# The opening of an attention-then-mixer kernel: which latents are scored first, and where the small copies stand

## The chip, the cores and the metric

The kernel runs on one core of one Trainium2 chip. The metric is device time in microseconds (us) of one execution; the time before is a median of 3 runs. TensorE (PE) multiplies matrices into PSUM, ScalarE (ACT) and VectorE (DVE) move and change results, GpSimd (POOL) and SyncE (SP) here mostly issue DMAs. PEld is TensorE's weight load, which overlaps its matmuls.

## The reference

For each of 8 batches, with sequence length S = 3136, width D = 256 and latent width 64:

```python
scores = (1 / S) * z @ z.T              # z: [8, 3136, 64]
attn   = np.maximum(scores, 0) ** 2
x      = u * (attn @ v)                 # u, v: [8, 3136, 256]
h      = x.transpose(0, 2, 1) @ U @ V   # U: [3136, 32], V: [32, 3136]
y      = x + h.transpose(0, 2, 1)
out    = y + np.maximum(y @ w_ch1, 0) @ w_ch2   # w_ch1: [256, 1024], w_ch2: [1024, 256]
```

## The kernel before

**Tiles.** The 3136 rows are cut into 25 tiles of 128, the last with 64 rows (`NT` = 25, `NF` = 24, `TAIL` = 64). "Latent j" is tile j of z; "output o" is tile o of the result. Since scores are symmetric, for every latent j the kernel keeps only its blocks with the tiles j to j + 12 (cyclically) in `A[j]` (up to 13 blocks of 128 columns); the other 12 blocks that output o needs are a transposed copy of `A[o]`, made by a DMA on SP (`turn`, L398) into a buffer called `strip`.

**A score step** (`score`, L353) takes two halves of a block row. Two matmuls (L360) in different 64-row halves of the array write the two halves of one PSUM pair tile (`pair_psum`, two buffers of two banks). ACT applies the ReLU and the scale into `A` (L378), or DVE does it where the argument `vector` says so (L374), and then DVE squares the block in place (L380). `make_stored` calls `score` for a panel of blocks of two latents; `score_steps` cuts a whole row of `A` into steps.

**An attention step** multiplies blocks by tiles of `v` (`half`, L478), two outputs at a time, accumulating in two sets of two PSUM banks (`sets`). `close_pair` (L487) adds the two banks (an ACT copy, L492, and a DVE sum, L493) and multiplies by `u` (DVE, L510). The tile of `u` comes by a DMA on POOL (`load_u`, L462), into one of two buffers, `u_sb`.

**After a batch**, the low-rank part runs inside the next batch: `rank_sums` (L580), `rank_close` (L592, L594), and `low_rank` (L635), which multiplies a tile of `V_bf` by the rank-32 sums. `V_bf` holds four copies of V in the four 32-row groups, and consecutive matmuls of `low_rank` read its rows 0 to 63 and 64 to 127. In the stretch of outputs of batch 0, the steps in `puts` fill it: DVE writes the first group in six steps (L332, L339) and then two copies (L343) widen it from 32 to 64 and from 64 to 128 rows.

**Order.** The schedule is manual: the program's order is the order of each engine's queue. For the steady state, `attend_steps` gives the matmuls of one output, and `_spread` and `_merge` put the score steps of coming latents between them. The first batch has its own opening, `start_up`, which does outputs 12 to 19 (12 is `FIRST`, 16 is `LEAD`) before the loop over outputs begins with i = 8 (output 20; `turns(i)` is (12 + i) mod 25).

- `first_z` issues dummy matmuls (L269) on a zeroed tile while z arrives, then casts z to bf16, one copy on DVE (L277) and one on ACT (L278). `turn_on_pe` transposes latents on PE with an identity (L285) and copies them out of PSUM into `zT_first` (L293).
- Outputs 12 to 15 are done together: for each entry of `pairs`, `make` scores two latents against tiles 12 to 15 and, two entries later, `use` multiplies those blocks by `v`. Into the gaps go the score steps of latents 16 to 19 (`nxt`), some on DVE (`vector`). The latents 16 to 24 are turned at entry 6.
- Outputs 16 to 19 follow the same way from stored blocks (`make_stored`, `use_stored`). The products by `u` of the first four outputs (`products`) and the loads of the next two pairs of `u` tiles stand between the two groups, followed on POOL by a one-column copy (`mark`, L886), which waits for a strip, and two loads of the next batch's `v`.
- `first_at`, `first_more` and `first_turns` say which score steps and turns go into outputs i = 8 to 14.

```python
        pairs = [(8, 9), (10, 11), (12, 13), (14, 15), (6, 7), (3, 4), (5,), (1, 2)]
        pairs += [(0, 16), (17, 18), (19, 20), (21, 22), (23, 24)]
        ...
        for i, pair in enumerate(pairs):
            ...
            make(pair)
            if i > 5 and i % 2:
                nxt.pop(0)()
            if i > 1:
                use(pairs[i - 2], outs)
```

Of the kernel before, what the change touches and what calls it, by code (L numbers as in the profile page):

```python
# [42 lines left out]
def kernel(  # L43
# [218 lines left out]
    def first_z(parts):  # L262
# [5 lines left out]
        for _ in range(7):  # L268
            mm(out=ps[:, 0, :], lhsT=zT_rest[:, 0, :], rhs=wide, start=True, stop=True)  # L269
        landed = []  # L270
        for t0, t1 in parts:
            z_f = u_pool.tile([P, 2, D], FP32, name="u_sb").rearrange("p a c -> p (a c)")
            z_f = z_f.rearrange("p (t c) -> p t c", c=dqk)
            nc.sync.dma_start(out=z_f, in_=rows(z[0])[:, t0:t1, :])
            landed.append(z_f)
        for (t0, t1), z_f in zip(parts, landed):
            nc.vector.tensor_copy(out=z_bf[:, t0:t1, 0, :], in_=z_f)  # L277
            nc.scalar.copy(out=z_bf[:, t0:t1, 1, :], in_=z_f)  # L278

    def turn_on_pe(parts, banks):  # L280

        z_bf = z_two
        for (t0, t1), ps in zip(parts, banks):
# [8 lines left out]
            copy = nc.vector.tensor_copy if t0 % 8 or t1 == NF else nc.scalar.copy  # L292
# [21 lines left out]
    def weight_steps():  # L314
# [26 lines left out]
        def copies():  # L341
            for n in (R, 2 * R):
                nc.vector.tensor_copy(out=V_bf[n : 2 * n, :], in_=V_bf[:n, :])  # L343
# [4 lines left out]
        return fetches, second_w, puts + [put_tail, copies]  # L348
# [4 lines left out]
    def score(b, parts, vector=False):  # L353
# [18 lines left out]
        for dst, src in todo:  # L372
            if vector:
# [5 lines left out]
        for dst, _ in todo:  # L379
            nc.vector.tensor_tensor(out=dst, in0=dst, in1=dst, op=ALU.mult)  # L380

    def score_steps(b, j, k0=0, k1=NB, vector=()):
# [5 lines left out]
        for i in range(parts):  # L388
            at = k0 * P + i * each

            def step(at=at, i=i):
                dst = A[j][:, at : at + each].rearrange("p (i h) -> p i h", i=2)
                score(b, [(j, j * P + at + k * h, h, dst) for k in range(2)], i in vector)
# [387 lines left out]
    def start_up():  # L781
        parts = ((8, 16), (0, 8), (16, NF))
        first_z(parts[:2])
# [9 lines left out]
        )  # L793
        load_v(0, (8, 12))
        load_v(0, (12, 18))
        load_z(0, parts[2:])
        for part in [(3, 8), (0, 3), (18, NF), (NF, NT)]:
            load_v(0, part)
        turn_on_pe([(8, 12), (12, 16)], sets[0])
        turn_on_pe([(0, 4), (4, 8)], sets[1])  # L800
# [12 lines left out]
        vector = {LEAD: (1,), LEAD + 1: (0,)}  # L813
# [3 lines left out]
        pairs = [(8, 9), (10, 11), (12, 13), (14, 15), (6, 7), (3, 4), (5,), (1, 2)]  # L817
# [3 lines left out]
        def make(pair):  # L821
            if all(LEAD - 1 - HALF <= j < FIRST for j in pair):
# [5 lines left out]
                score(0, todo)  # L828
            else:
# [3 lines left out]
                score(0, [(j, c0, NG * P, room) for j in pair])  # L833
# [8 lines left out]
        for i, pair in enumerate(pairs):  # L842
            if i == 4:
                double_z(parts[2:])
            if i == 6:
                turn_on_pe([(16, NF)], [pair_psum().rearrange("p a w -> p (a w)")])
                turn_on_pe([(NF, NT)], [pair_psum()[:, 0, :]])
                extend_z(0)
            make(pair)
            if i > 5 and i % 2:  # L850
                nxt.pop(0)()
            if i > 1:
                use(pairs[i - 2], outs)
# [28 lines left out]
        run(products)  # L882
        for o in outs[::2]:
            load_u(0, o)
        if B > 1:
            nc.gpsimd.tensor_copy(out=mark, in_=strips[0, LEAD + NG - 1][:, 0, :1])  # L886
            for part in V_PARTS[3:5]:
                load_v(1, part)
# [5 lines left out]
        for i, pair in enumerate(pairs):  # L894
# [5 lines left out]
            if i == len(pairs) - 1:  # L900
                turn(0, LEAD + NG)
        tail = []
# [16 lines left out]
        for s in _merge(tail, more[:-2] + rest[:2] + more[-2:]):  # L919
            s()  # L920
        turn(0, LEAD + 2 * NG - 1)


# [9 lines left out]
    for j, i in zip(range(3, FIRST), (10, 11, 12, 13, 13, 13, 14, 14, 14)):  # L933
        first_at[i].append((j, 0, FIRST - j))
    first_more = {
        8: [((j, j - 1), LEAD + NG) for j in (LEAD - 5, LEAD - 7)] + [((LEAD - 1, LEAD - 2), LEAD + 2 * NG)],
        9: [((LEAD - 3, LEAD - 4), LEAD + 2 * NG)],
    }
    first_turns = {8: (), 9: (24,), 10: (0,), 11: (1,), 12: (2,), 13: (3,), 14: ()}
# [152 lines left out]
```

## Time and profile before

| what | value |
|---|---|
| median of 3 runs | 998.56 us (994.47 to 998.61) |
| the profiled execution | 994.09 us, its span 992.4 us |
| PE busy | 979.3 us (99%), 13632 instructions |
| PEld busy | 814.9 us (82%) |
| ACT busy | 613.9 us (62%) |
| DVE busy | 554.5 us (56%) |
| POOL busy | 170.1 us (17%) |
| granted TensorE clock | 1.000 |

The span runs from the first to the last recorded instruction, and the 1.7 us between it and the execution's time lie around it. A matmul's end is modelled, so a busy PE is not a PE at its peak pace. Idle time of an engine costs something only where the engine that sets the end waits for it. The profile's line numbers are those of the kernel before.

### The profile page before, as it was taken

The numbers are of one execution on the slowest core, as the hardware profiler recorded it, in microseconds if no ns is written. First come the engines' busy times: TensorE is split into PE (matmuls) and PEld (weight loads), VectorE is DVE, ScalarE is ACT, GpSimd is POOL, SyncE is SP. The second block draws the span as 40 slices with busy tenths as digits, with TensorE's granted clock in tenths as the row PEclk, the third lists the DMA queues.
The fourth block names the chain that finished last, engine by engine and source line by source line (L and its number), as shares of the span: only waits on it lengthen the run. The fifth ranks groups of instructions, "written<-read, shape, count | busy, mean of one in ns | idle before, by whom it ended". The sixth has DMA issues, their size and how long they took to land.

```text
span 992.4 us, 31020 instructions
## 1 busy us (share of the span) xinstructions
PE 979.3 (99%) x13632; PEld 814.9 (82%) x13672; DVE 554.5 (56%) x1027; ACT 613.9 (62%) x843; POOL 170.1 (17%) x317
## 2 busy tenths in 40 slices
PE   8899999999999999999999999999999999999998
PEld 5788878888888888788887888878888788788876
DVE  6789835557346574374653655546546466352342
ACT  7879764766647575575755757467574676643154
POOL 5111112112121111212112121121211201111000
PEclk9999999999999999999999999999999999999999
DMA  9999889999799899998987999989889796595443
GB/s 197 175 175 210 149 172 207 176 193 180 140 186 182 164 174 138 194 184 167 171 161 167 187 169 164 164 169 188 160 159 194 157 192 127 126 199 109 89 107 102
DMA packets 399976, 164.42 MB, mean 166 GB/s; under 512 B 375568, under 2 KB 384464, under 8 KB 399840
## 3 DMA queue, kind: packets, MB, share of 16 engines
q1 hardware_dynamic: 371520, 96.14, 61.1%
q0 software_dynamic: 28320, 66.28, 28.1%
q8 instruction: 107, 1.75, 0.7%
q14 instruction: 29, 0.24, 0.1%
HBM read 61.88 MB, written 25.69 MB: 88 GB/s over the span
## 4 chain that ended last, share of the span: by engine, by line
PE 95%; ACT 2%; DVE 2%; issue 0%; DMA 0%; DVEq 0%
PE ps L478 50%; PE ps L714 17%; PE ps L667 17%; PE ps L360 7%; ACT A L378 2%; PE ps L635 1%; PE ps L525 1%; DVE A L380 1%; PE ps L580 1%; DVE x_bf L510 0%; PE ps L269 0%; DMA out_dram<-o_sb 0%; PE ps L285 0%; DVE both L493 0%; ACT both L492 0%
## 5 line engine op out<-in xcount | busy, mean ns | idle before, releaser
L378 ACT ACTIVATE A<-ps 128x832 bf16<-128x832 f32 (+10 forms) x479 | 356.7, 765 | 140.8 <-PE ps L360 135.2
L478 PE MATMUL ps<-v,A 64*128 64x256 bf16 x4988 | 341.2, 269 | 2.5 <-DVE A L380 2.5
L380 DVE TENSOR_TENSOR A<-A 128x832 bf16<-128x832 bf16 (+9 forms) x481 | 243.4, 523 | 131.5 <-ACT A L378 129.1
L478 PE MATMUL ps<-v,strip 64*128 64x256 bf16 x4420 | 309.5, 269 | 0.0
L478 PEld LDWEIGHTS <-A 64*128 64x128 bf16 x4988 | 252.1, 94 | 41.8 <-issue 6.0
L685 ACT ACTIVATE relu_bf<-ps 128x1024 bf16<-128x1024 f32 (+2 forms) x208 | 188.2, 909 | 150.4 <-PE ps L667 144.7
L478 PEld LDWEIGHTS <-strip 64*128 64x128 bf16 x4420 | 227.3, 94 | 30.5
L714 PE MATMUL ps<-w_bf,relu_bf 128*128 128x256 bf16 (+1 forms) x1600 | 201.4, 273 | 0.4
L667 PE MATMUL ps<-ut,w_bf 128*128 128x512 bf16 (+2 forms) x856 | 198.1, 353 | 1.7
L714 PEld LDWEIGHTS <-relu_bf 128*128 128x128 bf16 (+1 forms) x1600 | 153.0, 98 | 40.2 <-issue 4.9
L732 DVE TENSOR_TENSOR o_sb<-ps,x_bf 128x512 f32<-128x512 f32 (+2 forms) x81 | 54.9, 678 | 170.9 <-PE ps L714 164.6
L667 PEld LDWEIGHTS <-w_bf 128*128 128x128 bf16 x896 | 117.9, 144 | 37.4 <-issue 6.7
L360 PE MATMUL ps<-zT 64*128 64x416 bf16 (+8 forms) x812 | 134.8, 312 | 0.0
L462 POOL DMA_DIRECT2D u_sb<-in_u_dram x96 | 53.5, 557 | 453.4 <-DVE x_bf L510 430.5
L492 ACT COPY both<-ps 128x512 f32<-128x512 f32 (+1 forms) x104 | 59.0, 568 | 70.0 <-PE ps L478 63.9
L493 DVE TENSOR_TENSOR both<-ps,both 128x512 f32<-128x512 f32 (+1 forms) x104 | 69.3, 666 | 30.8 <-ACT both L492 30.4
L649 DVE TENSOR_TENSOR x_bf<-ps,x_bf 128x512 bf16<-128x512 f32 (+1 forms) x112 | 65.5, 626 | 11.3 <-PE ps L635 11.2
L510 DVE TENSOR_TENSOR x_bf<-both,u_sb 128x512 bf16<-128x512 f32 (+1 forms) x104 | 69.7, 671 | 3.6
L745 POOL DMA_DIRECT2D out_dram<-o_sb x66 | 36.0, 546 | 187.0 <-DVE o_sb L732 175.0
L360 PEld LDWEIGHTS <-zT 64*128 64x128 bf16 x812 | 46.3, 94 | 3.7
L732 DVE TENSOR_TENSOR both<-ps,x_bf 128x512 f32<-128x512 f32 (+1 forms) x24 | 15.0, 623 | 57.3 <-PE ps L714 57.3
L306 POOL DMA_DIRECT2D v<-in_v_dram x61 | 33.7, 555 | 4.0 <-issue 2.7
(66 smaller groups left out, 244.3 us busy)
## 6 DMA issues: line engine op xcount, KB each, us to landing
u_sb<-in_u_dram POOLq DMA_DIRECT2D x96, 256.0 KB, 4.4
out_dram<-o_sb POOLq DMA_DIRECT2D x66, 256.0 KB, 3.0
v<-in_v_dram POOLq DMA_DIRECT2D x57, 192.0 KB, 4.4
out_dram<-both POOLq DMA_DIRECT2D x18, 256.0 KB, 2.3
strip<-A SPq DMA_TRANSPOSE x194, 5.5
out_dram<-o_sb SPq DMA_DIRECT2D x11, 256.0 KB, 2.1
z_c<-in_z_dram POOLq DMA_DIRECT2D x7, 384.0 KB, 6.7
w_bf<-in_moe_w_ch_dram POOLq DMA_DIRECT2D x2, 512.0 KB, 6.2
```

What stands on the lines that cost most here:

```text
L360: mm(out=ps[:, k, :n], lhsT=zT[halves[k], j + at[k], :], rhs=zT_flat[halves[k], c + at[k] * P : c + at[k] * P + n], start=True, stop=True,)
L378: nc.scalar.activation(out=dst, in_=src, func=AF.Relu, scale=sc)
L380: nc.vector.tensor_tensor(out=dst, in0=dst, in1=dst, op=ALU.mult)
L478: mm(out=acc[t0][h][:, (o - t0) * D : (o - t0 + 1) * D], lhsT=w[halves[h]], rhs=v_both[b % 2][halves[h], j, :], start=start, stop=stop, **kw,)
L492: nc.scalar.copy(out=both[:, :w], in_=banks[1][:, :w])
L493: nc.vector.tensor_tensor(out=both[:, :w], in0=banks[0][:, :w], in1=both[:, :w], op=ALU.add)
L510: nc.vector.tensor_tensor(out=x_at(b, t0, n), in0=split(both[:, :w]), in1=u_sb[:, :n, :].rearrange("p t (a c) -> p t a c", c=P), op=ALU.mult,)
L649: nc.vector.tensor_tensor(out=q, in0=split(ps[h][:, : len(ks) * D]), in1=q, op=ALU.add)
L667: mm(out=ps[i][:, :w] if apart else ps[:, i, :w], lhsT=w1_at[:, db, hp + i, :], rhs=uT[c][:, db, len(chunks[c]) * P - w :], start=(db == 0 ...
L685: nc.scalar.activation(out=relus[c][:, hp : hp + 2, :w], in_=ps[:, :, :w], func=AF.Relu)
L714: mm(out=ps[r, k * D : (k + 1) * D], lhsT=relus[c][:, ht, q : q + (TAIL if two else P)], rhs=w2_bf[:, ht, :], start=(ht < 1 + two), stop=( ...
L732: nc.vector.tensor_tensor(out=o_sb[:p].rearrange("p t (a c) -> p t a c", c=P), in0=split(ps[:p, k0 * D : (k + 1) * D]), in1=x_at(b, t, nk) ...
```

## The change

The change touches the order of work in the opening and the place of two copies; the matmuls that make the result are the same.

- z arrives in three parts instead of two (tiles 12 to 15, 8 to 11, 0 to 7). The tiles 12 to 15 are cast and turned first, then 8 to 11. There is one dummy matmul less.
- The entries (12, 13) and (14, 15) move to the front of `pairs`. The tiles 0 to 7 are cast after the first entry and turned after the second. In the first entry, latent 13 is evicted by DVE from the second half of the pair tile whose first half ACT evicts, and both squares stand behind the cast. The products of the first use are split by pairs of outputs.
- At entry 6, tile 24 is turned first, then 16 to 19 (copied by ACT) and 20 to 23 (by DVE), both into one pair tile.
- At entry 9 the `nxt` step comes ahead of the squares. The second step of latent 18, instead of the first of latent 17, is evicted by DVE.
- The products by `u` of outputs 12 to 15, the two loads of `u`, `mark` and the two loads of `v` move behind the fourth entry of the second group.
- The last steps of the opening: all four panels for outputs 20 to 23 are scored there (two of them came in output i = 8 before); the two steps of latent 23 move to i = 8, and its turn behind it; the panels for 24 to 27 move from i = 8 and 9 to 9 and 10.
- The two copies that widen `V_bf` move from one step at i = 22 of batch 0 to the end of outputs i = 0 and i = 1 of batch 1.

```diff
@@ first_z
-        for _ in range(7):
+        for _ in range(6):
             mm(out=ps[:, 0, :], lhsT=zT_rest[:, 0, :], rhs=wide, start=True, stop=True)
...
+        def cast(n):
+            (t0, t1), z_f = parts[n], landed[n]
             nc.vector.tensor_copy(out=z_bf[:, t0:t1, 0, :], in_=z_f)
             nc.scalar.copy(out=z_bf[:, t0:t1, 1, :], in_=z_f)
@@ weight_steps
-        def copies():
-            for n in (R, 2 * R):
-                nc.vector.tensor_copy(out=V_bf[n : 2 * n, :], in_=V_bf[:n, :])
+        def copies(n):
+            nc.vector.tensor_copy(out=V_bf[n : 2 * n, :], in_=V_bf[:n, :])
@@ score
-        for dst, src in todo:
-            if vector:
+        for n, (dst, src) in enumerate(todo):
+            if n in vector:
...
-        for dst, _ in todo:
-            nc.vector.tensor_tensor(out=dst, in0=dst, in1=dst, op=ALU.mult)
+        def squares():
+            for dst, _ in todo:
+                nc.vector.tensor_tensor(out=dst, in0=dst, in1=dst, op=ALU.mult)
+        if held is None:
+            squares()
+        else:
+            held.append(squares)
@@ start_up
-        parts = ((8, 16), (0, 8), (16, NF))
-        first_z(parts[:2])
+        parts = ((12, 16), (8, 12), (0, 8), (16, NF))
+        on_act, on_dve = nc.scalar.copy, nc.vector.tensor_copy
+        cast = first_z(parts[:3])
...
-        turn_on_pe([(8, 12), (12, 16)], sets[0])
-        turn_on_pe([(0, 4), (4, 8)], sets[1])
+        cast(0)
+        turn_on_pe([(12, 16)], sets[0][:1], [on_act])
+        cast(1)
+        turn_on_pe([(8, 12)], sets[0][1:], [on_dve])
...
-        vector = {LEAD: (1,), LEAD + 1: (0,)}
+        vector = {LEAD: (1,), LEAD + 2: (1,)}
...
-        pairs = [(8, 9), (10, 11), (12, 13), (14, 15), (6, 7), (3, 4), (5,), (1, 2)]
+        pairs = [(12, 13), (14, 15), (8, 9), (10, 11), (6, 7), (3, 4), (5,), (1, 2)]
...
             if i == 6:
-                turn_on_pe([(16, NF)], [pair_psum().rearrange("p a w -> p (a w)")])
-                turn_on_pe([(NF, NT)], [pair_psum()[:, 0, :]])
+                turn_on_pe([(NF, NT)], [pair_psum()[:, 0, :]], [on_act])
+                ps = pair_psum()
+                turn_on_pe([(16, 20), (20, NF)], [ps[:, 0, :], ps[:, 1, :]], [on_act, on_dve])
                 extend_z(0)
-            make(pair)
-            if i > 5 and i % 2:
-                nxt.pop(0)()
+            held = []
+            make(pair, vector=(1,) if i == 0 else (), held=held)
+            if i == 0:
+                cast(2)
+            if i == 1:
+                turn_on_pe([(0, 4), (4, 8)], sets[1], [on_dve, on_act])
+            if i == 9:
+                nxt.pop(0)()
+                run(held)
+            else:
+                run(held)
+                if i > 5 and i % 2:
+                    nxt.pop(0)()
             if i > 1:
-                use(pairs[i - 2], outs)
+                for some in (outs[:2], outs[2:]) if i == 2 else (outs,):
+                    use(pairs[i - 2], some)
...
-        run(products)
-        for o in outs[::2]:
-            load_u(0, o)
-        if B > 1:
-            nc.gpsimd.tensor_copy(out=mark, in_=strips[0, LEAD + NG - 1][:, 0, :1])
-            for part in V_PARTS[3:5]:
-                load_v(1, part)
...
+            if i == 3:
+                run(products)
+                for o in outs[::2]:
+                    load_u(0, o)
+                if B > 1:
+                    nc.gpsimd.tensor_copy(out=mark, in_=strips[0, LEAD + NG - 1][:, 0, :1])
+                    for part in V_PARTS[3:5]:
+                        load_v(1, part)
...
-        for s in _merge(tail, more[:-2] + rest[:2] + more[-2:]):
+        for s in _merge(tail, more[:-2] + rest):
             s()
-        turn(0, LEAD + 2 * NG - 1)
+        return more[-2:]
@@ after start_up
     first_more = {
-        8: [((j, j - 1), LEAD + NG) for j in (LEAD - 5, LEAD - 7)] + [((LEAD - 1, LEAD - 2), LEAD + 2 * NG)],
-        9: [((LEAD - 3, LEAD - 4), LEAD + 2 * NG)],
+        9: ((LEAD - 1, LEAD - 2), LEAD + 2 * NG),
+        10: ((LEAD - 3, LEAD - 4), LEAD + 2 * NG),
     }
-    first_turns = {8: (), 9: (24,), 10: (0,), 11: (1,), 12: (2,), 13: (3,), 14: ()}
+    first_turns = {8: (23,), 9: (24,), 10: (0,), 11: (1,), 12: (2,), 13: (3,), 14: ()}
...
-    puts = dict(zip((17, 18, 19, 20, 21, 22), puts))
+    puts = dict(zip((17, 18, 19, 20, 21), puts))
+    puts.update({NT + i: s for i, s in enumerate(copies)})
...
-            if b == 0 and i in puts:
-                puts[i]()
+            if b * NT + i in puts:
+                puts[b * NT + i]()
```

## The prediction

> **What bounds the kernel now.** I read the page first: which engine is busy, and what the chain that ended last is made of.
>
> ```profile
> PE 979.3 (99%) x13632; PEld 814.9 (82%) x13672; DVE 554.5 (56%) x1027; ACT 613.9 (62%) x843; POOL 170.1 (17%) x317
> ...
> PE 95%; ACT 2%; DVE 2%; issue 0%; DMA 0%; DVEq 0%
> ```
>
> TensorE sets the end, and the change takes no matmul away but one dummy. So it can win only TensorE's idle time. Busy time by stretch says where that is (start:end, length, PE, PEld, DVE, ACT, POOL).
>
> ```profile
> 0.00:20.00 20.00, 16.90 (x193) 11.58 (x194) 12.81 (x25) 14.79 (x22) 13.18 (x29) 1.00 0.98 195
> 20.00:40.00 20.00, 17.17 (x257) 13.52 (x253) 16.21 (x32) 16.86 (x27) 2.39 (x5) 1.00 1.08 177
> 40.00:60.00 20.00, 18.99 (x324) 15.73 (x320) 15.24 (x34) 17.40 (x31) 3.20 (x6) 1.00 0.98 164
> ...
> 80.00:100.00 20.00, 19.24 (x332) 17.11 (x330) 19.09 (x36) 17.99 (x25) 3.09 (x5) 1.00 1.22 218
> 100.00:200.00 100.00, 99.74 (x1396) 82.49 (x1397) 56.57 (x106) 63.42 (x85) 19.56 (x36) 1.00 0.98 173
> ```
>
> PE is idle for 3.1, 2.8, 1.0 and 0.8 us in the first, second, third and fifth row: 7.7 us, of which 1.3 lie before its first instruction. Later 0.26 us in 100 are left. The waits of PE up to 60 us, and then one up to 250 us, name the causes (total, times, longest):
>
> ```profile
> PE ps L360 <- ACT A L378: 2.5, 4, 0.8
> PE ps L478 <- DVE A L380: 1.7, 3, 0.9
> PE ps L360 <- DVE A L374: 0.7, 2, 0.4
> PE ps L360 <- ACT relu_bf L293: 0.4, 1, 0.4
> ...
> PE ps L478 <- DVE A L380: 0.8, 1, 0.8
> ```
>
> Scores wait for a free pair tile, which ACT or DVE empties; products wait for a square. The rest is read in the timeline (start, length, instruction, idle time before it).
>
> ```profile
> 1.26 3.17 PE L269 MATMUL ps<-zT 128*128 128x512 bf16 x7 [1.26 <-DVE zT L266]
> ...
> 4.28 1.89 PE L285 MATMUL ps<-x_bf 128*128 128x128 bf16 x16
> ...
> 6.75 4.88 ACT L378 ACTIVATE A<-ps 128x512 bf16<-128x512 f32 x8 [0.39 <-PE ps L360]
> ...
> 8.10 1.05 PE L478 MATMUL ps<-v,A 64*128 64x256 bf16 x16
> ...
> 12.58 0.68 PE L285 MATMUL ps<-x_bf 128*128 128x128 bf16 x9
> ...
> 47.30 0.28 PE L478 MATMUL ps<-v,A 64*128 64x256 bf16 x2 [0.86 <-DVE A L380]
> ...
> 95.14 2.00 DVE L343 COPY V_bf<-V_bf 32x3200 bf16<-32x3200 bf16 x2
> ...
> 99.66 0.83 PE L478 MATMUL ps<-v,A 64*128 64x256 bf16 x12 [0.76 <-DVE A L380]
> ...
> 108.50 0.69 DVE L510 TENSOR_TENSOR x_bf<-both,u_sb 128x512 bf16<-128x512 f32 x1
> ...
> 108.80 0.38 PE L635 MATMUL ps<-t_sb,V_bf 64*128 64x256 bf16 x4
> ```
>
> To be seen: 16 turns back to back from 4.43 (0.109 us each), ACT's score evictions from 6.75 with no gap until 11.63, the first product at 8.10, and the three places outside the first 40 us that matter below.
>
> **Up to entry 6: later, not earlier.** From the rows: ACT starts 512-wide evictions 0.48 us apart and 1024-wide ones 0.90 (eight in 4.88), one alone lasts 0.60 and 1.02; an ACT copy of 512 from PSUM takes 0.59, a cast 0.62; on DVE a cast takes 0.43, a copy from PSUM 0.69, squares 0.35 apart; a score pair holds PE 0.2, the 16 products of an entry 0.87. A 256-wide cast is an estimate between the 128-wide ACT copy (0.27) and the 512-wide cast: 0.4. Six dummies end at 4.0 (7 x 0.427 to 4.43), which hides the smaller first part of z. Four turns end at 4.44, and ACT copies them until 5.1. But ACT's second cast stands behind that copy and ends at 5.4, and PE's turns of 8 to 11 stand ahead of the first scores: these go out at 5.85, against 6.17. In the built program DVE's eviction of latent 13 waits for ACT's of latent 12 (6.4 to 7.0), as both read one pair tile: 7.05 to 7.75. DVE's cast of tiles 0 to 7 follows until 8.1, and PE's next eight turns wait for it: idle from about 6.5 to 8.15. They end at 9.0, the first products come at 9.25 against 8.10, and the fourth entry leaves ACT at 11.6 against 10.7, since ACT has done a cast and a copy between. At entry 6 the turns of 16 to 19 wait until ACT has emptied their pair tile (13.85); those of 20 to 23 wait for ACT's copy of the other half (15.0). Latent 5 is scored at 15.5, against 13.61: 1.9 us late.
>
> **Entries 7 to 12, and outputs 16 to 19: most of it won back.** From here one step is as before, but the step of latent 17 goes to ACT, whose 0.74 replace DVE's 1.02 and its wait (0.4 at 23.61), and at entry 9 the eviction comes ahead of a 0.69 square (0.26 at 20.44). Stepping the same durations through, the first product of (23, 24) comes at 25.7 instead of 24.84: 0.9 late. In the second group ACT sheds one 0.74 eviction; DVE's 1.02 for it comes behind a 0.69 sum and holds the next score pair: about even with what was won. The two products by u (1.29 on DVE) no longer stand ahead of squares for which PE waited 0.43 at 33.40. That point comes at 34.1. So this part costs **0.7 us**. I bound it by -2.5 (of the 5.9 us of idle in the first two rows, 1.3 is before the first instruction and some 2 are the filling of the pipeline) and +3 (the 1.9 kept, and the sum and the eviction in full).
>
> **u, v and SP.** The products move to about 36.5, where DVE had 1.1 us free. The loads of u behind them on POOL go out at about 37 to 38 instead of 32.70, and land after 4.4 us (median of the page) by 42.5; the first is needed at about 42.9. Cover 0.4: if gone, DVE is held, and with it squares; 0 to +1. `mark` and two loads of v move with them, and nothing else stands behind these on POOL before 43; that v is used after 99. On SP a third load of z costs 0.4 of issue; it lands (2.9 from issue) by 4.6, and is cast at 7. The turn of latent 23 has three outputs of time.
>
> **Outputs from 20 on.** The 0.86 wait at 47.30 was for a panel of latents 11 to 8 whose evictions came behind ACT's copy and whose squares behind two DVE operations of a closing pair. Now these panels are scored ahead of the closing: **-0.9**. What is late next is latent 23, which isn't needed for three outputs. 0 if the u loads hold DVE.
>
> **V's copies.** 95.14's 2.0 us held squares, and PE waited 0.76: **-0.8**. The first copy, 1.0, now falls at 103.7, into idle time of DVE (0.9 and 0.4 in a row there). The second stands behind output i = 1, that is behind the product at 108.50 (ends 109.2), and lasts until 110.2. But `low_rank` reads rows 64 to 127 with its second matmul at 108.8, and all PE's work stands behind it in order: **+1.4**. It is 0 if that output comes later relative to DVE, +2 if DVE is behind.
>
> **Sum.** 0.7 - 0.9 - 0.8 + 1.4 = +0.4 on the profiled execution: 994.09 becomes 994.5. That execution is at the lower end of the runs shown (998.61, 994.47, 998.56; the median 4.5 above it). The middle of all four is 996.5, and I put the forecast there: 997.
>
> **A rule against the change.** Row first: dummies and turns run at 0.427 and 0.109 us for 512 and 128 columns, later a 512-wide pair holds PE 0.2, and nine turns at 12.58 take 0.62 in the chain: PE's pace doubles between 6.2 and 7.9, though the granted clock reads 1.00 throughout. The Trainium skill, "TensorE: Matmul & The Clock Gate", section "The HAM clock gate", says that the clock is halved until a free-running window of about 3.4 us was busy. Before, PE was busy from 1.26 to 7.05 without a gap; the change opens gaps of 1.0 and 1.7 us just there. By the row alone the sum stays at +0.4. By the rule one such window could fail, and the sum would be that of the slower rival below.
>
> **The rivals.** *Faster:* the order does what its heading says, and the waits of the first 60 us go. From idle times: 2.8 + 1.0 in the second and third row, 0.4 for the dummy, 0.8 at 99.66, and no wait in `low_rank`: -5.0, 991.5. For it: PE's waits are all short and of the kind that order mends. Against it: the chain above puts ACT and DVE casts ahead of the first products. *Slower:* PE stays at the slow pace until 12.6, because of the two gaps. The work from 8.15 on (eight turns 0.9 at the slow pace already, four entries of 0.87, five score pairs of 0.2) is 4.5 us at the fast pace and 9 at the slow: +4.5, and +4.9 with the sum, 1001.4; it decides from the second product entry on. Against it: part of this would lie in waits. *The copies find room:* `low_rank` doesn't wait, and the sum is -1.0; within the forecast.
>
> **How the numbers follow.** A measurement of this kernel can tell about 0.5%, 5 us, from no change. Forecast (no change that can be told) 0.66; faster 0.18, which includes a median that falls to the runs' lower end; slower 0.16. The range goes from the lower runs with the opening's best bound (994.3 - 2.5, about 991.5) to the higher with the sum of the upper bounds that I believe together (998.6 + 3.4 = 1002).
>
> **What would show it.** Right: first score at about 5.9, first L488 matmul (the products by v) after 9, an idle PE of 1.5 us or more ahead of the turns of tiles 0 to 7, latent 5 scored after 15, no wait near 47 and 99, and one of over 1 us in `low_rank`'s first call near 109. Wrong: first products before 8.1, or PE's idle time in the first 40 us under 4 us (then faster), or turns of 0.1 us each at entry 6 (then slower).

## The result and the profile after

The changed kernel takes 1007.81 us (median of four runs, 1004.74 to 1009.66), against 996.76 for the kernel before (four runs, 994.47 to 998.61). The ratio is 1.0103, with an interval of 1.0055 to 1.0152: slower by about 1%, 11 us, where no change was forecast. The kernel before runs in two groups, most executions near 994 us and about a third between 997 and 1005, so its medians, and the ratios to them, depend on how many of each a series has. The profiled execution took 1006.45 us with a span of 1004.7, against 994.09 and 992.4. That is 12.3 us more to explain.

The page of the changed kernel, its busy times and its chain:

```profile
PE 986.0 (98%) x13671; PEld 816.8 (81%) x13671; DVE 555.4 (55%) x1030; ACT 613.9 (61%) x845; POOL 170.7 (17%) x317
...
PE 95%; ACT 2%; DMA 2%; DVE 1%; issue 0%
```

Two things are new. PE is busy 6.7 us longer, though it has a dummy less to do. And DMA, 0% of the chain before, has 2%. The stretches tell where (PEclk, third from the end, is the granted clock):

```profile
0.00:20.00 20.00, 15.52 (x144) 9.57 (x145) 10.37 (x23) 11.82 (x21) 12.26 (x27) 1.00 0.90 174
20.00:40.00 20.00, 17.82 (x258) 13.32 (x258) 17.64 (x33) 17.91 (x28) 2.08 (x4) 1.00 0.90 145
40.00:60.00 20.00, 13.20 (x174) 9.81 (x172) 9.13 (x19) 9.57 (x18) 3.87 (x8) 0.83 1.14 130
...
80.00:100.00 20.00, 20.00 (x357) 17.83 (x355) 17.55 (x38) 16.87 (x29) 2.83 (x5) 1.00 1.26 211
100.00:200.00 100.00, 98.71 (x1375) 82.83 (x1371) 59.10 (x112) 64.05 (x87) 18.88 (x34) 1.00 0.97 178
```

The third row is the large one: PE is idle for 6.8 us instead of 1.0, and the granted clock falls to 0.83. The first row has 1.4 us more idle time and a quarter fewer matmuls. In the row from 80 us the idle time of before is gone. The waits of PE up to 60 us, and from there to 250:

```profile
PE ps L488 <- DMA strip<-A: 6.7, 2, 5.9
PE ps L290 <- DVE x_bf L280: 1.4, 1, 1.4
...
PE ps L290 <- ACT x_bf L281: 1.0, 1, 1.0
PE ps L290 <- ACT relu_bf L297: 0.7, 1, 0.7
...
PE ps L645 <- DVE V_bf L346: 1.2, 1, 1.2
```

The last three of the first group and the wait for `V_bf` were forecast. The first line was not: products of the second group wait for a DMA transpose of a panel into a strip. PE's timeline of the changed kernel shows both ends of the trouble:

```profile
5.42 0.61 PE L290 MATMUL ps<-x_bf 128*128 128x128 bf16 x4 [0.98 <-ACT x_bf L281]
5.95 1.04 PE L363 MATMUL ps<-relu_bf 64*128 64x512 bf16 x4
8.40 1.01 PE L290 MATMUL ps<-x_bf 128*128 128x128 bf16 x8 [1.41 <-DVE x_bf L280]
...
9.74 1.92 PE L488 MATMUL ps<-v,A 64*128 64x256 bf16 x16
...
13.74 1.04 PE L488 MATMUL ps<-v,A 64*128 64x256 bf16 x16
...
17.54 0.39 PE L363 MATMUL ps<-relu_bf 64*128 64x512 bf16 x1
...
52.92 0.61 PE L488 MATMUL ps<-v,strip 64*128 64x256 bf16 x4 [5.91 <-DMA strip<-A]
...
53.66 2.13 PE L488 MATMUL ps<-v,strip 64*128 64x256 bf16 x18
```

The same 16 products take 1.92 us at 9.74 and 1.04 at 13.74: PE is at half pace until about 13.4. And after the wait of 5.91 it is at half pace again: 18 products take 2.13 us, where 16 take 1.04. In finer stretches of the same kernel:

```profile
48.00:52.00 4.00, 0.00 (x0) 0.00 (x0) 1.25 (x2) 0.00 (x0) 1.60 (x3) 0.87 1.51 101
52.00:56.00 4.00, 3.08 (x28) 2.12 (x30) 0.59 (x1) 0.86 (x1) 0.00 (x0) 0.50 1.06 80
```

PE does nothing for four microseconds; then the granted clock is 0.50. The Trainium skill, "TensorE: Matmul & The Clock Gate", section "The HAM clock gate", says that PE's clock halves after an idle window of about 3.4 us; this trace agrees, with an idle time of 5.9 us and a clock of 0.50 behind it. It can take less: in "no `mark`" below, the longest wait is 2.6 us, and the granted clock from 50 to 53 us is 0.50 too.

What the DMAs did that were issued between 40 and 42 us (KB each, us to landing):

```profile
v<-in_v_dram POOLq DMA_DIRECT2D x2, 192.0 KB, 8.5
...
strip<-A SPq DMA_TRANSPOSE x1, 12.2
```

In the kernel before, strip 20's transpose went out at 38.10 and landed 4.0 us later. Here it goes out at 40.72 and takes 12.2; strip 21's, at 43.02, takes 15.7. The u loads (38.94 and about 39.5) and the v loads (40.19 to 41.7) go out just ahead of it: 2 x 256 KB and 2 x 192 KB, 896 KB together. Before, these had gone out from 32.70 on and taken 3.2 and 4.0 us.

The sum along PE's timeline: the first score of latent 20 comes at 37.76 instead of 35.21 (+2.55). Then 6.7 of waits for strips. From 52.92 to 57.64 PE does 38 products and two score pairs in 4.7 us; at 0.0545 a product and 0.2 a pair they are 2.5, so 2.2 for the pace. The wait near 47 is gone (-0.86), and so is the one near 99 (-0.76); the one in `low_rank` has come (+1.2). That is +11.0 of the 12.3 us; the rest is in no single wait.

### The profile page after: what moved, and what is told of

It reads as the page before. It is cut to its first block, busy times and chain, and to the rows that moved or that the text cites. A ratio compares the mean times of both kernels' runs of the same rounds, so it can differ in the third digit from the quotient of the medians.

```text
span 1004.7 us, 31064 instructions
## 1 busy us (share of the span) xinstructions
PE 986.0 (98%) x13671; PEld 816.8 (81%) x13671; DVE 555.4 (55%) x1030; ACT 613.9 (61%) x845; POOL 170.7 (17%) x317
## 4 chain that ended last, share of the span: by engine, by line
PE 95%; ACT 2%; DMA 2%; DVE 1%; issue 0%
PE ps L488 50%; PE ps L677 17%; PE ps L724 17%; PE ps L363 7%; DMA strip<-A 2%; ACT A L381 1%; PE ps L645 1%; PE ps L535 1%; PE ps L590 1%; PE ps L290 0%; PE ps L269 0%; DVE A L385 0%; ACT both L502 0%; DVE both L503 0%; DVE A L377 0%
## 5 line engine op out<-in xcount | busy, mean ns | idle before, releaser
L488 PEld LDWEIGHTS <-strip 64*128 64x128 bf16 x4420 | 228.7, 94 | 38.3 <-DMA strip<-A 7.4
L677 PE MATMUL ps<-ut,w_bf 128*128 128x512 bf16 (+2 forms) x896 | 201.5, 355 | 0.0
```

What stands on the lines that cost most here:

```text
L488: mm(out=acc[t0][h][:, (o - t0) * D : (o - t0 + 1) * D], lhsT=w[halves[h]], rhs=v_both[b % 2][halves[h], j, :], start=start, stop=stop, **kw,)
L677: mm(out=ps[i][:, :w] if apart else ps[:, i, :w], lhsT=w1_at[:, db, hp + i, :], rhs=uT[c][:, db, len(chunks[c]) * P - w :], start=(db == 0 ...
```

## The experiments

Each was timed beside runs of the kernel before on the same chip; ratios are to these. "The changed kernel" is the one above.

**Loads early.** Is it the moved loads? This is the changed kernel with that one block put back.

```diff
+        run(products)
+        for o in outs[::2]:
+            load_u(0, o)
+        if B > 1:
+            nc.gpsimd.tensor_copy(out=mark, in_=strips[0, LEAD + NG - 1][:, 0, :1])
+            for part in V_PARTS[3:5]:
+                load_v(1, part)
         rest = [
...
-            if i == 3:
-                run(products)
-                for o in outs[::2]:
-                    load_u(0, o)
-                if B > 1:
-                    nc.gpsimd.tensor_copy(out=mark, in_=strips[0, LEAD + NG - 1][:, 0, :1])
-                    for part in V_PARTS[3:5]:
-                        load_v(1, part)
```

> The changed kernel, with one block put back where it stood before: the two products by u, the two loads of u, the mark and the two loads of v between the two groups of outputs. Theory A (the 896 KB of loads, issued at 38.9 to 41.7 instead of 32.7 to 36.5, share the DMA engines with the transpose of latent 20's strip, which lands 12.2 us after its issue instead of some 5): the 5.9 us wait for a strip goes, and with it the slow pace behind it; the strip lands in 4 to 6 us, and the time falls by 8 to 9 us, to about 998, 2 to 4 us above the kernel before. Theory B (the strip is late because of the other reordering at the end of the opening, four panels and a turn moved): the wait stays at 4 us or more and the time at 1005 or above.

997.33 us, ratio 1.0024 (1.0001 to 1.0047). No wait for a strip; strips land in 3.8 to 5.9 us. The block costs 0.8%, some 8 us, and 2 to 3 us are left. What is left lies mostly in the first 15 us (two experiments below test this), where this profile shows the pace also as a clock (products in the timeline, then the stretch):

```profile
8.92 1.91 PE L488 MATMUL ps<-v,A 64*128 64x256 bf16 x16
```

```profile
8.00:10.00 2.00, 2.00 (x22) 1.29 (x24) 1.90 (x5) 1.58 (x4) 1.61 (x4) 0.62 1.10 204
```

The changed kernel's row for the same stretch reads 1.00, though its products from 9.74 us on took nearly twice their time. In an opening the durations of matmuls are the better witness.

**Only the loads late.** The kernel before, with that block alone moved (the same diff the other way).

> The kernel before, with only that block moved as in the change (behind the fourth entry of the second group). Theory A: PE waits 4 to 7 us for a strip at about 45, and the time is 6 to 10 us longer than before. Theory B: no wait for a strip, and the time is that of before within 1 us (0.4 less by the wait at 33.4).

1002.3 us, ratio 1.0064 (1.0043 to 1.0085). The waits of PE up to 60 us, and the DMAs issued between 37 and 39:

```profile
PE ps L478 <- DMA strip<-A: 6.0, 2, 3.7
```

```profile
v<-in_v_dram POOLq DMA_DIRECT2D x2, 192.0 KB, 9.0
strip<-A SPq DMA_TRANSPOSE x1, 10.3
```

The block by itself brings the wait, 6.0 us, and most of the loss (0.64% of 1.03%). The opening isn't needed for it.

**u or v, or both, or their order?** Seven kernels vary the loads, all from the changed kernel: "v first" (`mark` and v back in their old place, u late), "v later still" (`mark` and v behind the opening's last steps), "u early, v beside" (u early, `mark` reading latent 20's first square), the same with `mark`'s copy done three and six times, "v behind" (`mark` reading strip 20), and "no `mark`".

```diff
 v later still (v first: the same lines ahead of "rest = [")
         for s in _merge(tail, more[:-2] + rest):
             s()
+        if B > 1:
+            nc.gpsimd.tensor_copy(out=mark, in_=strips[0, LEAD + NG - 1][:, 0, :1])
+            for part in V_PARTS[3:5]:
+                load_v(1, part)
 u early, v beside the strip (three and six copies: that copy in a loop)
+        run(products)
+        for o in outs[::2]:
+            load_u(0, o)
         rest = [
...
+            if i == 4 and B > 1:
+                nc.gpsimd.tensor_copy(out=mark, in_=A[LEAD + NG][:, :1])
+                for part in V_PARTS[3:5]:
+                    load_v(1, part)
 v behind the strip: mark and v moved behind the loop, with
+            nc.gpsimd.tensor_copy(out=mark, in_=strips[0, LEAD + NG][:, 0, :1])
 no mark
-                    nc.gpsimd.tensor_copy(out=mark, in_=strips[0, LEAD + NG - 1][:, 0, :1])
```

First, v:

> The changed kernel, with the mark and the two loads of v back between the groups, and the products and the loads of u left behind the fourth entry. Tells which load does it. If the 384 KB of v do most: the wait for a strip falls below 2 us and the time to about 999. If the 512 KB of u do: it stays at 3 us or more and the time at 1003 or above. If only the sum of both counts: in between, 1 to 3 us of wait.

> The changed kernel with one thing moved: `mark` and the two v loads of 192 KB go still later, to the end of the opening (some 65 to 70 us), while the u loads stay beside the second group. Theory (the loss is the collision of 896 KB of loads with the transposes of strips 20 and 21, not the lateness of the loads): the strips land in about 4 to 8 us, PE has no wait over 0.5 us for a strip near 50, its granted clock stays at 1.00 in 40 to 60 us, and the kernel takes about 998 us, as with v early and u late (998.2, ratio 1.0024), 8 us or so less than the changed kernel. Rival 1 (any v load that comes late costs): the same 7 to 8 us loss, or a new wait. Rival 2 (v collides with the strips of the tail of the opening instead): a strip wait of 1 us or more between 65 and 85 us, 1000 to 1005 us.

Then u early, v as close as in the changed kernel, and v held behind the strip. (In the first of these u, out at 35.95, lands only at 41.7 and 42.4, so it is still in flight when strip 20's transpose goes out at 41.36.)

> The changed kernel with the products and the u loads early (as in the first experiment), and `mark` made to read the first square of latent 20, so that the two v loads go out at about 39 to 40 us, within a microsecond ahead of strip 20's transpose, as they did in the changed kernel, while the u loads have landed long before. Theory (the v loads, issued just ahead of the transposes, are what holds these up): strips 20 and 21 land in 10 us or more, PE waits 3 to 6 us for one near 48 to 53, the granted clock falls behind that, and the kernel takes 1003 to 1008 us. Rival (it takes u and v together, 896 KB): the strips land in 7 us or less, no PE wait over 1 us there, and the time is 997 to 998 us, as in the first experiment.

> The changed kernel with `mark` made to read strip 20 instead of strip 19, so that the two v loads cannot go out before strip 20 has landed; the products and the u loads stay late. Theory (the transposes lose only to v loads that are ahead of them or with them): strip 20 lands in about 5 us, v goes out at about 46 us, PE has no wait over 1 us for a strip up to 60 us, and the kernel takes about 998 us, ratio near 1.0025. Rival (strips 21 and 22 are caught instead, since their transposes stand behind strip 20's on SP): a strip lands in 10 us or more, a PE wait of 2 us or more between 50 and 62 us, 1001 to 1005 us.

And then the order of issue:

> The kernel with u early and v held by a square of latent 20, with that small copy on POOL done three times instead of once: v's two loads go out some 0.3 to 0.6 us later, so that strip 20's transpose (41.36 there) falls ahead of the second or of both. With one copy it took 997.6 us and strips landed in 6.4 to 7.3 us. Theory (order of issue: a transpose issued ahead of a v load moves side by side with it, and both crawl): strip 20 or 21 lands in 10 us or more, v takes 8 us or more instead of 4.3, PE waits 3 to 6 us for a strip, 1003 to 1008 us. Rival (u must be in flight as well): strips in 6 to 8 us, no wait over 1 us, 997 to 998 us.

> The same with the small copy done six times: v's loads go out about 0.8 to 1.2 us later than with one, both behind strip 20's transpose at 41.36 and ahead of strip 21's at about 43.2. Theory (order of issue): strip 20's packets move side by side with v's; strip 20 or 21 lands in 10 us or more, and the time is 1003 to 1008 us. Rival 1 (u must be in flight as well): 997 to 998 us, strips in 8 us or less. Rival 2 (the transpose is ahead far enough to win): strip 20 in 5 us, strip 21 in 7 to 8, 997 to 998 us, and v in 5 us or more.

> The changed kernel without the one-column copy into `mark` (0.65 us on POOL in its profile; the v loads keep their place behind the late u loads). The v loads go out some 0.1 to 0.5 us sooner, both ahead of strip 20's transpose (40.72). Theory (order of issue): v lands in 4 to 5 us, strips in 6 to 8 us, PE has no wait over 1 us for a strip, and the time is about 998 us: one small copy decides over 8 us. Rival (896 KB late, in this order, is what does it, whatever comes first): strips in 10 us or more, a wait of 4 to 6 us, 1004 to 1008 us.

What was measured, from each kernel's timeline and DMAs (first issue of u, v and of strip 20's and 21's transposes, and these two's landing, in us):

| kernel | u | v | strips 20, 21 out | landing | us, median | ratio (interval) |
|---|---|---|---|---|---|---|
| before | 32.70 | 35.45 | 38.10, 39.98 | 4.0, 5.6 | | 1 |
| changed | 38.94 | 40.19 | 40.72, 43.02 | 12.2, 15.7 | 1007.81 | 1.0103 (1.0055 to 1.0152) |
| loads early | 34.51 | 37.19 | 39.91, 42.26 | 5.0, 5.4 | 997.33 | 1.0024 (1.0001 to 1.0047) |
| only loads late | 35.76 | 37.41 | 37.45, 39.67 | 10.3, 14.5 | 1002.30 | 1.0064 (1.0043 to 1.0085) |
| v first | 39.66 | 38.62 | 40.69, 42.74 | 6.4, 7.1 | 998.21 | 1.0024 (1.0001 to 1.0047) |
| v later still | 39.15 | 46.74 | 40.91, 42.88 | 4.9, 5.7 | 997.88 | 1.0029 (1.0009 to 1.0049) |
| u early, v beside | 35.95 | 40.69 | 41.36, 43.24 | 6.4, 7.3 | 997.64 | 1.0025 (1.0001 to 1.0048) |
| v behind | 37.74 | 44.76 | 39.50, 41.53 | 5.0, 5.7 | 997.85 | 1.0011 (0.9988 to 1.0034) |
| three copies | 35.98 | 41.34 | 41.39, 43.27 | 6.8, 7.4 | 997.45 | 1.0013 (0.9988 to 1.0038) |
| six copies | 34.55 | 41.21 | 39.96, 41.84 | 3.8, 9.8 | 1002.21 | 1.0052 (1.0026 to 1.0078) |
| no `mark` | 38.38 | 39.51 | 40.14, 42.37 | 8.9, 12.2 | 1001.04 | 1.0040 (1.0014 to 1.0067) |

In two of these the edit didn't bring the times it was meant to. In "v first", `mark` waits for strip 19, which lands only at 38.3, so v isn't early; and "v later still" goes out at 46.7, not at 65, since POOL runs ahead of PE's work. Both tell something all the same.

What the table shows: in every kernel with a landing of 8.9 us or more, a v load goes out within 0.7 us of one of the transposes (six copies: v at 41.2 and 41.8, strip 21 at 41.84). Where v is over 1.5 us ahead of strip 20's or behind both, the landing is 7.1 us or less, whether u is late or not, and PE doesn't wait. So lateness costs nothing, and u's loads alone, some 1 us ahead of the transposes in "v later still" and "v behind", did no harm. The six copies show that v alone can do it: u had landed at 40.9.

What falls: that v beside a transpose is enough ("u early, v beside" and "three copies" were as close, and their strips landed in 6.4 to 7.4 us); that u must be there too (six copies); that all four loads near the transpose are enough (v first: all within 2.1 us ahead, 6.4); and that the order of issue decides (three copies: the transpose went out between the two v loads, and landed in 6.8; no `mark`: behind both, 8.9 and 12.2). Taking `mark` away brought the loss from 1.0% to 0.4%, not to 0.25. So it is shown that the place of these loads makes the strips late, and which places kept clear of it here; what decides near a transpose is open.

Nor is v the only load that can do it. "V's copies" below keeps the loads in their old order, and in its profile strip 19's transpose goes out at 31.55, u's first load 0.7 us behind it and v's only at 42.45:

```profile
strip<-A SPq DMA_TRANSPOSE x1, 10.2
```

Late strips turn up far from the moved loads, too: in the profile of "v first" PE waits 2.3 us for one at 129 us, in that of the six copies 3.1 us at 81. Whether such waits make the upper group of the kernel before is not shown.

How the two queues share the time can be seen (packets, MB, time of the packets as a share of 16 engines; q0 is POOL's loads, q1 SP's transposes). In the changed kernel from 44 to 45 us, then in "u early, v beside" from 43 to 44 and from 45 to 46:

```profile
q0 software_dynamic: 63, 0.08, 68.7%
q1 hardware_dynamic: 141, 0.04, 47.2%
```

```profile
q0 software_dynamic: 76, 0.10, 88.8%
...
q1 hardware_dynamic: 873, 0.22, 106.9%
q0 software_dynamic: 28, 0.02, 14.4%
```

In the first kernel both queues move packets from 43 us on, and neither gets far; in the second v's loads go first, and then the transposes go fast. The other kernels of the table divide in the same way: with a landing of 8.9 us or more the queues run side by side for at least four microseconds, with under 450 transpose packets in each; in the rest the transposes reach 450 or more within two microseconds of their first packets. What starts the one or the other isn't shown.

The slowness lasts. The transposes' queue from 48 to 49 us in the changed kernel, and from 46 to 47 in "u early, v beside", where v had landed:

```profile
q1 hardware_dynamic: 280, 0.07, 110.9%
```

```profile
q1 hardware_dynamic: 1130, 0.28, 133.0%
```

The recorded time on transposes is about the same in both, on a quarter of the packets: some 63 ns for each against 19. By then the changed kernel's POOL queue moves only 18 packets in that microsecond, and the other kernel's none. So the transposes don't merely stand in line behind v: their own packets take longer, and still do when few loads are left.

**Old start.** What of the rest is the start? The first experiment's kernel with its first 15 us as before; the transfers of z, the first loads of v (which the change had reordered too) and the turns of entry 6 go back with the lines shown.

```diff
-        parts = ((12, 16), (8, 12), (0, 8), (16, NF))
+        parts = ((8, 16), (0, 8), (16, NF))
...
+        turn_on_pe([(8, 12), (12, 16)], sets[0])
+        turn_on_pe([(0, 4), (4, 8)], sets[1])
...
-        pairs = [(12, 13), (14, 15), (8, 9), (10, 11), (6, 7), (3, 4), (5,), (1, 2)]
+        pairs = [(8, 9), (10, 11), (12, 13), (14, 15), (6, 7), (3, 4), (5,), (1, 2)]
```

> The changed kernel with u's and v's loads back between the two groups of score blocks (as in the first experiment, which took 997.3 us), and with its first 15 us as before: z in two transfers, scores of latents 8 to 15 in rising order, all four turns ahead of the first score, v in its first parts of before. The order of the panels, of latent 23, of the DVE half steps and of V's two copies stays changed. Theory (what is left of the loss in the first experiment is the start: two entries at a slow pace and two gaps): PE's first 16 products take about 1.05 us again, the scores of latent 20 come about 2.5 us earlier than in the changed kernel, and the kernel takes 994 to 995 us, within 0.1% of the kernel before, since the two waits near 47 and 99 are gone (-1.6) and low_rank's wait of 1.2 is there. Rival (the rest of the reorder costs it): 997 us, as the first experiment.

994.81 us, ratio 0.9983 (0.9958 to 1.0007); span 992.6 against 994.7 of the first experiment. Latent 20's first score comes at 34.23 us: 2.8 before the first experiment's 37.02, and 1.0 before the kernel before's 35.21. From latent 5 (13.58) to latent 20 it takes 20.65 us, against 21.60 in the kernel before (13.61 to 35.21). So the orders of entry 9 and of the DVE half steps, which the change had made, gain about 1 us together, and the start loses more than that. Here v (37.18) again goes out beside strip 20's transpose (37.12): it lands in 7.1 us, and PE waits 0.8 us for it near 44.

**Busy gaps.** Is it the pace? The first experiment's kernel with dummy matmuls in the two gaps of PE.

```diff
+        def busy(n, bank):
+            for _ in range(n):
+                mm(out=bank[:, :], lhsT=zT_rest[:, 0, :], rhs=wide, start=True, stop=True)
...
         cast(1)
+        busy(2, sets[1][0])
         turn_on_pe([(8, 12)], sets[0][1:], [on_dve])
...
             if i == 1:
+                busy(3, sets[1][0])
                 turn_on_pe([(0, 4), (4, 8)], sets[1], [on_dve, on_act])
```

> The first experiment's kernel (loads early, changed start, 997.3 us) with dummy matmuls that fill PE's two gaps of the start: two ahead of the turns of tiles 8 to 11, three ahead of the turns of tiles 0 to 7, into a bank that is free. Theory (the gaps keep PE at the slow pace until 13.4 us): PE is at full pace by about 8 us, the first 16 products take about 1.05 us instead of 1.9 and the next 16 about 1.05 instead of 1.45, and the kernel takes 1 to 2 us less, near 996. Rival (the slow pace has nothing to do with the gaps): the 16 products still take 1.9 us, and the time is that of the first experiment or up to 1 us more, for the dummies.

995.36 us, ratio 0.9992 (0.9976 to 1.0008), span 993.1. PE's timeline:

```profile
6.26 0.82 PE L285 MATMUL ps<-zT 128*128 128x512 bf16 x3
...
8.72 1.11 PE L492 MATMUL ps<-v,A 64*128 64x256 bf16 x16
...
14.77 0.39 PE L367 MATMUL ps<-relu_bf 64*128 64x512 bf16 x1
```

Five dummies more, and the products take 1.11 us instead of 1.91 from the first entry on. Latent 5 is scored at 14.77 instead of 16.36, latent 20 at 35.43 instead of 37.02. Both are 1.6 us earlier, and against the changed kernel's own profile (17.54 and 37.76), whose half pace lasted longer, 2.8 and 2.3. In all nine profiles with the changed start and without these dummies the first 16 products take 1.91 or 1.92 us; in both with them, 1.11. So the half pace is most of what the start cost. The ratios point the same way (1.0024 before, 0.9992 now), though their intervals overlap. At full pace the changed opening is only 0.2 us behind the kernel before at latent 20, but 1.2 behind the old start with the same later orders.

**V's copies.** First the kernel before with V's two copies alone at the changed places:

```diff
-        return fetches, second_w, puts + [put_tail, copies]
+        return fetches, second_w, puts + [put_tail], [lambda n=n: copies(n) for n in (R, 2 * R)]
...
+    puts.update({NT + i: s for i, s in enumerate(copies)})
```

> The kernel before, with only the two copies that widen V moved to the ends of outputs 0 and 1 of batch 1. One look, for two waits: the 0.76 us wait for squares near 99 goes, and the first low-rank product near 108 waits for the second copy, 1.2 to 1.5 us. Net +0.4 to +0.8, too little for the time to show. The rival (the copies find room) expects no wait near 108.

994.74 us in a single run (span 993.0). The wait near 99 is gone and one of 1.2 for `V_bf` has come. Then two kernels with the copies one output sooner: the old start's, and the kernel with busy gaps.

```diff
-    puts.update({NT + i: s for i, s in enumerate(copies)})
+    puts.update({NT - 1 + i: s for i, s in enumerate(copies)})
```

> The kernel with the start of before and the loads early, and with V's two copies put one output sooner: at the ends of the last output of batch 0 and of the first output of batch 1. Theory (each copy is 0.73 us or so on DVE and hides when low_rank's second matmul has an output's time behind it, and the first no longer queues with the second): no PE wait over 0.3 us for V_bf, none near 99, and about 1 us less than with the copies at the ends of the first and second outputs of batch 1, 993 to 994 us. Rival (DVE is short at the end of batch 0, as in the kernel before with both copies): a PE wait of 0.5 to 0.8 us near 99 comes back, and the time is the same.

> The kernel with the changed start, its two gaps filled with dummy matmuls, and the loads early, with V's two copies put one output sooner (ends of the last output of batch 0 and of the first of batch 1). The kernel without that last edit took 995.4 us (0.9992 of before) and has a PE wait of 1.2 us for V_bf; with the start of before the same edit took the ratio from 0.9983 to 0.9969. Theory: the wait goes, and the time is about 1 us less, 994 to 994.5 us, ratio near 0.998. Rival (the start of before is worth more than the profile shows): the time is within 0.5 us of the other start with the same copies, near 0.997. Since the two stand 1 us apart, the run decides chiefly whether the wait for V_bf goes here too.

With the old start: 994.19 us, ratio 0.9969 (0.9945 to 0.9993). With busy gaps: 994.04, 0.9984 (0.9972 to 0.9997). Neither has any wait of PE between 60 and 250 us. The copies themselves, in the first of them (ns of one, first and last start):

```profile
L342 DVE COPY V_bf<-V_bf x2: 983/986/989, 99.9 to 102.0; 32x3200 bf16<-32x3200 bf16 x1, 64x3200 bf16<-64x3200 bf16 x1
```

They end at 103, and `low_rank` comes at 106.7. Both intervals lie just below 1, by 0.3 and 0.2%. Much of that is the kernel before's upper group: against the median of its runs under 996.5 us, 994.3 and 994.1 beside these two, they are only some 0.1 us shorter. So both clearly beat the changed kernel, and the kernel before hardly. How the two starts compare can't be told, as the intervals overlap.

**End of the opening and copies alone.** The kernel before, with the order of the last panels and of latent 23 as in the change, and the copies one output sooner.

```diff
-        for s in _merge(tail, more[:-2] + rest[:2] + more[-2:]):
+        for s in _merge(tail, more[:-2] + rest):
             s()
-        turn(0, LEAD + 2 * NG - 1)
+        return more[-2:]
...
+    puts.update({NT - 1 + i: s for i, s in enumerate(copies)})
```

> The kernel before with two parts of the change alone: the order of the last panels and of latent 23 at the end of the opening, and V's copies one by one, at the ends of the last output of batch 0 and of the first of batch 1. Theory (these are the parts that remove the waits of 0.86 us near 47 and 0.76 us near 99, and nothing else of the change is needed for it): both waits gone, no wait for V_bf, about 1.5 us less than the kernel before. Rival (the waits move: the panels' casts or the copies are late for the next user): the time within 0.5 us of the kernel before, with a new PE wait of 0.5 us or more near 50 to 60 or near 103.

992.96 us, ratio 0.9982 (0.9962 to 1.0003). Both waits are gone, near 47 and near 99, with none for `V_bf`. Its span is 1.3 us shorter than that of before, and its median 1.4 us below that of the lower group of before beside it (994.3), though the interval just includes no change. A wait of 0.6 us for a strip near 44 has come, where v (37.42) goes out with strip 20's transpose (37.44). Its start is the code of before, and yet PE's timeline reads

```profile
4.17 1.12 PE L285 MATMUL ps<-x_bf 128*128 128x128 bf16 x16
```

where the same 16 turns took 1.89 in the profile of before. Latent 5 is scored at 12.95 instead of 13.61, so some 0.7 us of the shorter span are luck of this profile. The point at which PE gets its full pace moves between executions, by more than a microsecond: with the changed start it came at about 12 us in the first experiment's profile and at about 13.4 in the changed kernel's. The Trainium skill, "TensorE: Matmul & The Clock Gate", section "The HAM clock gate", says that the window in which PE's activity is counted runs freely; these numbers agree.

## Why the prediction was wrong, point by point

**"u, v and SP": the step that failed.** It asked two things of the moved loads: whether u lands in time (cover 0.4, if gone 0 to +1), and whether anything stands behind them on POOL ("nothing else stands behind these on POOL before 43; that v is used after 99"). Both answers held. The third question wasn't asked: which transfers that PE does wait for are in flight at the new place? Strip 20's transpose goes out on SP at 40.72, on another queue, within 0.6 us of both v loads. All landing times were taken from medians of the page, as if they were fixed. The term of 0 to +1 was about +8: ratio 1.0103 with the block late and 1.0024 without, and in the changed kernel's profile 6.7 of waits and 2.2 of pace. No rival named it, so the range ended at 1002, 6 us short. What decides near a transpose is open, but in the experiments v did no harm 1.5 us or more ahead of strip 20's transpose, or 3 us or more behind strip 21's.

The Trainium skill, "DMA: Bandwidth & Descriptors", section "Queues, rings and completion order", says that each DMA engine takes turns, packet by packet, between the queues that have work for it. The landing of 12.2 us beside 896 KB of loads agrees that queues share engines; no run here shows the turns themselves.

**"Up to entry 6" and "Entries 7 to 12": the pace was left out of the sum.** The schedule was as worked out: first score at 5.95 (5.85), turns of tiles 0 to 7 after a gap of 1.41, first product at 9.74 (9.25). But the sum stepped full-pace durations, and latent 5 came at 17.54, not 15.5. Two entries that took 1.92 and 1.81 instead of 1.05 are 1.6 of these 2.0 us. The recovery behind it was about right: the start was 3.9 us late at latent 5 and 2.55 at latent 20, so 1.4 were won back, against 1.2 forecast. With the busy gaps the two points are 1.15 and 0.2 late, against 1.9 and 0.7. So this term, forecast at +0.7 and bounded by +3, measured about +2.5, and nearly all of that, 2.3, goes with the busy gaps; in the first experiment's profile, where the half pace was shorter, it was 1.6.

**The slower rival** was right in its mechanism and its end (PE at half pace until about 13.4, for 12.6) and too dear: the pace cost 1.6 to 2.8 us at latent 5, not 4.5. Part of the slow work did lie in waits for DVE and ACT, as was said against it. It was made a rival of the whole sum, though, where it should have stood in the sum.

**"Outputs from 20 on": right.** The wait of 0.86 is gone in every run with the new order of panels.

**"V's copies": right.** -0.76 near 99, and a wait of 1.2 in `low_rank` for a forecast of 1.4. One output sooner there is neither.

**The faster rival** fell at once: the idle time of the first two stretches grew from 5.9 to 6.7 us. But what it hoped for is there in the parts, as the kernels that keep the start, the loads' place and only the orders show.

## What to carry to other kernels

When a load is moved, look at what else is in flight at its new place on any queue, and take its landing time from that crowd, not from the page's median: a transfer with 2 us of slack can be late when other loads go out within a microsecond of it, though in several kernels here it wasn't. Hold a load that isn't urgent by letting it depend on the urgent transfer's landing; that cost one changed operand here. And keep PE busy until it is at full pace: a gap of 1 us in the first 8 us costs not that microsecond alone, but can cost a half-pace stretch behind it, which a few dummy matmuls avoid.

## What the runs showed of the hardware

- A transpose that lands in 4 to 6 us when loads keep clear takes 6.4 to 15.7 when two loads of 192 KB go out within 0.7 us of it. Where it is late, both queues move packets side by side for four microseconds or more, and a transpose's packet takes three times as long (63 ns against 19, in one microsecond of each kind). Which of the two ends it is isn't told by the bytes or by the order of issue. With two loads of 256 KB 0.7 and 1.3 us behind it, one took 10.2.
- A late transfer costs PE twice: the wait itself (5.9 us) and the half pace behind it (2.2 us), for the granted clock went from 1.00 to 0.50. A wait of 2.6 us was followed by 0.50 as well ("no `mark`").
- Two gaps of PE, 1.0 and 1.4 us, early in the program moved its full pace from between 6.2 and 7.9 us to about 13.4; with both gaps mostly filled, it was there by 8.7.
- The granted clock in the profile's rows can read 1.00 through half-pace matmuls at a program's start.
